# Four small moves between engines: zeroing, a product, a scaling and two factors in an attention and feed-forward kernel

## The chip, the core and the metric

The kernel runs on one core of a Trainium2 chip. The core has a matrix engine (TensorE, PE in the profile, with its weight loads shown apart as PEld), three engines that work on tiles element by element (VectorE, DVE; ScalarE, ACT; GpSimd, POOL) and a queue engine (SyncE, SP) that issues most transfers. Each engine works through its own list of instructions in order, and waits on semaphores for the others. Data lie in SBUF (128 partitions); TensorE writes its results to PSUM, from where VectorE or ScalarE take them.

The metric is the device time of one execution in microseconds (us), as the median of several runs. Lower is better.

## The reference

Two stages. The first is a linear attention with a decaying state, for 4 batches and 8 heads of 768 steps with 48 channels each; the second is a feed-forward block on the 3072 rows that come out, 384 wide, 1024 inside.

```python
def _attn_ref(r, k, v, w, u):
    ...
    for t in range(S):
        kt, vt, rt = (k[:, :, t], v[:, :, t], r[:, :, t])
        cur = np.einsum('bhd,bhe->bhde', u[None] * kt, vt)
        y[:, :, t] = np.einsum('bhd,bhde->bhe', rt, state + cur)
        state = w[None, :, :, None] * state + np.einsum('bhd,bhe->bhde', kt, vt)
    ...
def _moe_ref(x, w_in, w_out, g_ln):
    h = x @ w_in
    h_max = np.max(h, axis=-1, keepdims=True)
    e = np.exp(h - h_max)
    sm = e / (np.sum(e, axis=-1, keepdims=True) + 1e-09)
    solu = h * sm
    mu = np.mean(solu, axis=-1, keepdims=True)
    var = np.mean((solu - mu) ** 2, axis=-1, keepdims=True)
    ln = (solu - mu) / np.sqrt(var + 1e-06) * g_ln
    return (ln @ w_out).astype(np.float32)
```

`r`, `k`, `v`, `w`, `u` arrive in float32, the weights `w_in`, `w_out` and `g_ln` in float64. The part with `u` is what each step adds for itself; below it is called the own product: the sum over the channels of r times u times k, one number per head and step.

## The kernel before

**Chunks.** The 768 steps of each batch are cut into 6 chunks of 128. A chunk of one batch is a unit; there are 24, numbered 0 to 23, all batches of the first chunk first. A unit's `r`, `k` and `v` are loaded with the steps on the partitions (`rpad`, `kpad`, `vt`). The order of the instructions is written out by hand, for every engine: what a function issues stands on the engine's list where the function is called. Nothing reorders it.

**A unit's way.** `decay_k` (L718) multiplies `k` with a table of decays `kdec` on GpSimd and gives `kp`. `weigh` (L732) makes the own products on GpSimd in two multiplications, k times u (L734) and that times r (L735); `sum_own` (L737) sums them over the channels on VectorE; `diagonal` (L744) puts the sums on the diagonal of the score tile, on ScalarE for units 0 to 3 (L749), on GpSimd later (L754). `turn_r` and `turn_k` transpose `r` and `k` on TensorE; VectorE scales the first out of PSUM (L779), ScalarE copies the second (L788). `whole_scores` or `scores` multiplies the two on TensorE (L801, L819), `take_scores` puts the valid half of the result into the score tile on VectorE (L827, L832), and `whole_y` or `merged_y` multiplies that with `vt` (L858, L881). `take_y` (L892) copies the result to SBUF on ScalarE: it is the input `xT` of the feed-forward part. From unit 4 on, `vt` has two halves of 64 steps, with the running state in the rows that a half leaves free; so the second half, `vt[:, 1]`, must be zero where nothing is loaded. L641 zeroes it for all six `vt` tiles, on ScalarE, at the start.

**Feed-forward.** `ffn_in` (L962) multiplies with `w_in` on TensorE into one PSUM tile `h_ps` (L969); there is only one such tile, so the next unit's product waits until it has been read twice: by ScalarE's exponential (L977), and then by VectorE's L1053 in `unit_a`, which makes `solu` from it and the exponential. `unit_b` (L1057) takes sums of squares on ScalarE. Then come the variance, the root (`root`, L1075, on GpSimd) and two factors (`shifts`, L1079: a scale and a shift for each row), with which `normalise` (L1098, on ScalarE) finishes the row. `halve_ln` (L1124) splits its words into 16-bit halves on ScalarE and issues a transpose by DMA on SP; `join_ln` (L1130) puts the halves together again on VectorE (L1121). `row_sums_12` and `row_sums_34` make sums of the rows of two units (L1201 to L1207), and `both_a` to `both_d` multiply with `w_out`, two units at a time (L1211).

**The weights.** They arrive as float64 words and become float32 in 14 pieces, 0 to 5 of `w_in`, 6 to 13 of `w_out`. A piece takes four steps: `convert_a` (L531, ScalarE), `convert_b` (L540, VectorE, two instructions), `convert_c` (L556, GpSimd, L560), and for pieces of `w_out` `convert_d` (L563): a multiplication with `minus_g`, on VectorE (L571) for even pieces, on ScalarE (L568) for odd ones.

**The order around the change.** The start (L1313 to L1396) is written out. The transposes of unit 0 and of the decay table come first; ScalarE then copies the table out (`turn_table`, L665) and has in front of it the copy of `u` (L639) and the six zeroings (L641). On GpSimd come `ones` (L710), two small products `wide` (L1322) that wait for VectorE's tables, `weigh(0)`, `decay_k(0)`, and later `decay_k(1)` and `weigh(1)`. A loop of five turns follows (L1399, i from 2 to 6), in which every turn handles up to two pieces of `w_out`: the pieces taken up in one turn go through `convert_c` and `convert_d` in the next. Three more loops handle the middle, and the end (L1725 on) is written out again: there unit 23, the last, gets its `variance`, `root` and `shifts` alone, between the stages of units 18 to 22.

Of the kernel before, what the change touches and what calls it, by code (L numbers as in the profile page):

```python
# [9 lines left out]
F32 = mybir.dt.float32  # L10
# [389 lines left out]
def direct_path(  # L400
# [29 lines left out]
    nc = tc.nc  # L430
    B, H, S, D = r.shape
# [18 lines left out]
    apool = ctx.enter_context(tc.tile_pool(name="apool", bufs=2))  # L450
# [15 lines left out]
    NLD, NV = 5, 6  # L466
    rpads = [const.tile([128, H, P], F32, name=f"rpad{i}") for i in range(NLD)]
    kpads = [const.tile([128, H, P], F32, name=f"kpad{i}") for i in range(NLD)]
    vts = [const.tile([128, 2, H, P], F32, name=f"vt{i}") for i in range(NV)]

    def load(i, which="krv"):
        b, c = units[i]
        for t, src, n in ((kpads, k, "k"), (rpads, r, "r")):
            if n in which:
                nc.sync.dma_start(out=t[i % len(t)][:, :, 0:D],
                                  in_=src[b, :, ts(c, T), :].rearrange("h s d -> s h d"))
        if "v" in which:
            vt = vts[i % NV]
            for n, at, size in ((0, 0, T),) if i < WHOLE else ((0, 0, U), (1, U, U)):
                nc.sync.dma_start(  # L480
                    out=vt[at : at + size, n, :, 0:D],
                    in_=v[b, :, ds(c * T + at, size), :].rearrange("h s d -> s h d"))
# [57 lines left out]
    def convert_b(j):  # L540
        hi, low = step[j]
        n = low.shape[1]
        ma = wpool.tile([128, n], U32, tag="ma", name="ma", bufs=4)
        part = ma
        if pieces[j][2] is None:
            part = psM.tile([128, n], F32, tag="m", name="part").bitcast(U32)

        nc.vector.tensor_scalar(out=part, in0=hi, scalar1=3, scalar2=0x3FFFFFF8,  # L550
                                op0=ALU.logical_shift_left, op1=ALU.bitwise_and)
        nc.vector.scalar_tensor_tensor(out=ma, in0=hi, scalar=0xC0000000, in1=part,  # L552
                                       op0=ALU.bitwise_and, op1=ALU.bitwise_or)
        step[j] = ma, low
# [8 lines left out]
    def convert_d(j, scalar=False):  # L563
        dst, _, f = pieces[j]
        ma, low = step.pop(j)
        if f is not None:
            if scalar:
                nc.scalar.activation(out=dst, in_=ma.bitcast(F32), func=ACT.Copy,  # L568
                                     scale=minus_g[:, f : f + 1])
            else:  # L570
                nc.vector.tensor_scalar_mul(out=dst, in0=ma.bitcast(F32),  # L571
                                            scalar1=minus_g[:, f : f + 1])
# [64 lines left out]
    u_ps = psM.tile([128, dm], F32, tag="m", name="u_ps")  # L637
    nc.tensor.matmul(u_ps, ones_row, u_row, start=True, stop=True)
    nc.scalar.copy(out=u_bc.rearrange("p h d -> p (h d)"), in_=u_ps)  # L639
    for vt in vts:  # L640
        nc.scalar.activation(out=vt[:, 1].rearrange("p h x -> p (h x)"),  # L641
                             in_=ident[:, 0:1].to_broadcast([128, H * P]), func=ACT.Copy, scale=0.0)
    nc.vector.tensor_scalar(out=pw[:, 0, 0], in0=wd_ps, scalar1=LOW, scalar2=HIGH,
# [64 lines left out]

    ones = const.tile([128, 1], F32, name="ones")
    nc.gpsimd.memset(ones, 1.0)  # L710

    live = {}

# [4 lines left out]
    def decay_k(i):  # L718
        X = live.setdefault(i, {})
        X["kp"] = apool.tile([128, H, P], F32, name="kp", bufs=5)  # L720
        nc.gpsimd.tensor_mul(X["kp"].rearrange("p h d -> p (h d)"),  # L721
                             kpads[i % NLD].rearrange("p h d -> p (h d)"),
                             kdec.rearrange("p a d -> p (a d)"))
# [5 lines left out]
                             rpads[i % NLD].rearrange("p h d -> p (h d)"),  # L729
                             rdec.rearrange("p a d -> p (a d)"))  # L730

    def weigh(i, engine):  # L732
        rku = live[i]["rku"] = apool.tile([128, H, D], F32, name="rku")
        engine.tensor_mul(rku, kpads[i % NLD][:, :, 0:D], u_bc)  # L734
        engine.tensor_mul(rku, rku, rpads[i % NLD][:, :, 0:D])  # L735

    def sum_own(i):  # L737
        own = live[i]["own"] = small.tile([128, H, 1], F32, name="own")
# [35 lines left out]
    def turn_r(i):  # L774
        rT = factors(i)["rT"]
        ps = psM.tile([128, HP, T], F32, tag="m", name="tr_ps")
        for a in range(HP):
            nc.tensor.transpose(ps[:, a, :], pair(rpads[i % NLD], a), ident)
        nc.vector.tensor_mul(rT, ps, fore)  # L779
# [287 lines left out]
    def unit(i):  # L1067
        unit_a(i)
        unit_b(i)
# [9 lines left out]
    def shifts(i, j, engine):  # L1079
        i = max(i, SEVEN)  # L1080
        if i < j:
            tot, shift, scale, rstd = (stats[:, n, i:j] for n in (1, 2, 3, 4))
            engine.tensor_scalar(out=scale, in0=rstd, scalar1=-float(dff), scalar2=1.0,
                                 op0=ALU.mult, op1=ALU.mult)
            engine.tensor_tensor(out=shift, in0=tot, in1=rstd, op=ALU.mult)  # L1085
# [34 lines left out]
    def join(words, turned):  # L1120
        nc.vector.tensor_copy(out=words.bitcast(U16).rearrange("p n (t o) -> p o n t", o=2),  # L1121
                              in_=turned)
# [7 lines left out]
    def join_ln(i):  # L1130
        X = live[i]
        if i not in ROOM:
            X["lnT"] = fpool.tile([128, KF, 128], F32, name="lnT")
        else:
            X["lnT"] = bigs[ROOM[i]].rearrange("p (f t) -> p f t", f=KF)
        join(X["lnT"], X["turned"])
# [72 lines left out]
    def block(dst, rows, weights, start=False):  # L1209
        for f in range(KH):  # L1210
            nc.tensor.matmul(dst, rows[:, f], weights[:, f], start=(start and f == 0),  # L1211
                             stop=(f == KH - 1), skip_group_check=True)
# [52 lines left out]
    def both_c(i):  # L1265
        X, Y = live.pop(i), live.pop(i + 1)
        ending[i] = X
        o, o2, a, e = (X[n] for n in ("o", "o2", "a", "e"))
        rows, rows2 = (out[ds(b * S + c * T, T)] for b, c in (units[i], units[i + 1]))
        if not X.get("summed"):  # L1270
            nc.vector.tensor_tensor(out=o2[:, right], in0=a, in1=o2[:, right], op=ALU.add)
        block(a, Y["lnT"][:, KH:KF], sums_w[4])
        if i + 2 == N:
            nc.sync.dma_start(out=rows2[:, right], in_=o2[:, right])
        if X.get("summed") != 2:
            nc.vector.tensor_tensor(out=o[:, right], in0=e, in1=o[:, right], op=ALU.add)
        nc.sync.dma_start(out=rows, in_=o)
# [13 lines left out]
    def attend(chunks, at=0):  # L1291
        chunks = [i for i in chunks if i < N]
        scores(chunks, at)
        outer(chunks)
# [25 lines left out]
    for q in range(2):  # L1320
        rows = slice(q * P, q * P + D)
        nc.gpsimd.tensor_tensor(out=wide.rearrange("p (a q) -> p a q", q=2)[P : P + D, :, q],  # L1322
                                in0=back[rows, :, 0], in1=pw[rows, 0, 0], op=ALU.mult)
    weigh(0, nc.gpsimd)
    decay_k(0)
    sum_own(0)
    diagonal(0)
# [1 line left out]
    spin(2)  # L1329
    whole_scores(0)  # L1330
    convert_b(0)
    decay_k(1)
    weigh(1, nc.gpsimd)
    turn_r(1)
    spin(4)
# [63 lines left out]
    for i in range(LA, LA + LO):  # L1399
        j = i - LA  # L1400
        load(i + 5, "kr")
        load(i + 4, "v")
        if i > LA:
            ffn_in(j)
        before, now = now, [todo.pop(0) for _ in range(2 if todo else 0)]
        turn_r(i + 2)
        turn_k(i + 2)
        for p in before:
            convert_c(p)
        for p in now:  # L1410
            take_up(p)
        if i > LA:
            diagonal(i + 1)
            unit(j)
        for p in before:
            convert_d(p, p % 2)
        sum_own(i + 2)
        decay_k(i + 3)
        if i + 3 >= FIRST:
            decay_r(i + 3)  # L1420
        weigh(i + 3, nc.gpsimd)
        if i - LO >= 0:
            halve_ln(i - LO)
        if i - LO - 1 >= 0:
            join_ln(i - LO - 1)
        if i + 1 < WHOLE:
            whole_scores(i + 1)
            take_scores(i + 1)
        else:
            place(i + 1)  # L1430
            attend([i + 1])
            middle(i + 1)
        if LA < i < WHOLE:
            whole_y(i)
            take_y(i)
            whole_outer(i)
        elif i >= WHOLE:
            merged_y(i)
            take_y(i)
        if i > LA:  # L1440
            update(i)
        else:
            nc.vector.tensor_single_scalar(out=minus_g, in_=g_sb, scalar=-1.0, op=ALU.mult)
        if i + 1 >= WHOLE:
            take_scores(i + 1)
        for p in now:
            convert_b(p)
        halve_rk(i + 3)
# [17 lines left out]
    i = LA + LO  # L1466
    j, l = i - LA, 0
# [41 lines left out]
    for i in range(LA + LO + 2, ELEVEN, 2):  # L1509
        j, l = i - LA, i - LA - LO  # L1510
# [8 lines left out]
        first, second = ([n] if n < N else [] for n in (i + 2, i + 3))  # L1519
# [121 lines left out]
    for i in range(ELEVEN, N - 1, 2):  # L1641
        j, l = i - LA, i - LA - LO
        one, two = turned[i]
        first, second = ([n] if n < N else [] for n in (i + 2, i + 3))
# [80 lines left out]
    i = N - 1  # L1725
    j, l = i - LA, i - LA - LO
# [68 lines left out]
    variance(i, N, nc.vector)  # L1795
    root(i, N)
    both_c(l)
    shifts(i, N, nc.vector)
    join_ln(l + 3)
    row_sums_12(l + 2)  # L1800
    row_sums_34(l + 2, nc.vector)
    both_d(l)
# [72 lines left out]
```

## Time and profile before

| what | value |
|---|---|
| median of 5 runs | 322.94 us (321.71 to 323.35) |
| the profiled execution | 322.67 us, its span 320.9 us |
| granted TensorE clock | 0.998 |
| TensorE busy | 307.6 us (96%) |
| VectorE, ScalarE, GpSimd busy | 266.5 us (83%), 244.5 us (76%), 245.5 us (76%) |
| first product with `w_in` on TensorE (L969) | starts at 23.25 us |
| last matmul | ends at about 315 us |
| L641, zeroing on ScalarE | 6 of 0.62 us |
| L735, second own product on GpSimd | 24, median 1.01 us |
| L571, scaling on VectorE | 4, 0.47 to 0.73 us |
| L568, scaling on ScalarE | 4 of 0.60 us |

The profile is one execution. A line of its timeline gives the start in us from the begin of the span, the length in us, the engine, the line of the kernel, the operation, the tile written and the tiles read, their sizes, how many equal instructions were merged, and in brackets how long the engine was idle before and what ended that wait. "issue" stands for a wait for nothing that the profile shows.

### The profile page before, as it was taken

The page shows a single profiled execution, that of the slowest core. Times are in us where ns is not written, and L with a number is a line of the kernel's source. Part 1 is how long each engine was busy: PE and PEld are TensorE (multiplying, and loading weights), DVE is VectorE, ACT ScalarE, POOL GpSimd, SP SyncE. Part 2 cuts the span into 40 slices and gives each one's busy share as a digit, 9 for nine tenths or more (in the row PEclk, how much of TensorE's full clock was granted, in tenths as well). Part 3 has the DMA queues.
Part 4 walks back from the last instruction along what each step waited for, and adds up shares of the span by engine and source line. Part 5 has one row for each costly group of instructions (what it writes and reads, how often), then busy time and mean ns, then how long its engine had stood idle before and what let it go on. Part 6 is the DMA issues. An engine that isn't in the chain of part 4 may idle for free.

```text
span 320.9 us, 9696 instructions
## 1 busy us (share of the span) xinstructions
PE 307.6 (96%) x3903; PEld 217.1 (68%) x3903; DVE 266.5 (83%) x449; ACT 244.5 (76%) x418; POOL 245.5 (76%) x264
## 2 busy tenths in 40 slices
PE   5989999999999999999999999999999999999992
PEld 4966565555456466687677677667768677669892
DVE  7696999998887988989889799799979947677770
ACT  3885888888549888968968969949959968788420
POOL 4899778879999999999999999979988275272000
PEclk9999999999999999999999999999999999999999
DMA  8999998778999999988998999995876455575821
GB/s 172 246 257 194 206 183 198 132 134 143 190 165 179 172 171 154 162 146 171 161 201 170 173 182 218 206 194 87 163 182 140 78 133 116 128 198 118 189 89 61
DMA packets 165779, 52.62 MB, mean 164 GB/s; under 512 B 158301, under 2 KB 161502, under 8 KB 165726
## 3 DMA queue, kind: packets, MB, share of 16 engines
q1 hardware_dynamic: 165712, 51.92, 83.4%
q8 instruction: 32, 0.52, 0.7%
q14 instruction: 21, 0.17, 0.2%
q10 hardware_dynamic: 14, 0.00, 0.0%
HBM read 26.75 MB, written 4.72 MB: 98 GB/s over the span
## 4 chain that ended last, share of the span: by engine, by line
PE 64%; POOL 16%; DVE 11%; issue 4%; DMA 3%; POOLq 0%
PE o_ps L1211 26%; PE h_ps L969 18%; PE h_part L1003 9%; POOL kp L721 3%; POOL rku L734 3%; POOL rp L728 3%; POOL big L754 3%; PE y_ps L881 2%; PE at L819 2%; POOL rku L735 2%; DMA rpad<-in_r_dram 2%; DVE solu L1053 1%; PE h_part L881 1%; DVE ma L552 1%; PE y_ps L858 1%
## 5 line engine op out<-in xcount | busy, mean ns | idle before, releaser
L969 PE MATMUL h_ps<-w_in_sb,xT 128*128 128x512 f32 x216 | 96.9, 598 | 0.0
L969 PEld LDWEIGHTS h_ps<-w_in_sb,xT 128*128 128x128 f32 x216 | 39.9, 190 | 44.9 <-issue 42.9
L1127 ACT COPY halves<-solu 128x2048 uint16<-128x2048 uint16 x23 | 43.6, 1896 | 1.8 <-DMA halves<-halves 1.7
L721 POOL TENSOR_TENSOR kp<-kpad,kdec 128x512 f32<-128x512 f32 x24 | 34.1, 1423 | 1.3 <-ACT kdec L665 0.6
L1121 DVE COPY big<-halves 128x2048 uint16<-128x2048 uint16 x21 | 33.7, 1612 | 0.7 <-DMA halves<-halves 0.4
L1121 DVE COPY lnT<-halves 128x2048 uint16<-128x2048 uint16 x18 | 31.5, 1772 | 0.0
L735 POOL TENSOR_TENSOR rku<-rku,rpad 128x384 f32<-128x384 f32 x24 | 29.1, 1214 | 1.9
L832 DVE COPY_PREDICATED big<-later_half,at 64x512 f32<-64x512 uint32 x40 | 29.5, 736 | 0.7
L734 POOL TENSOR_TENSOR rku<-kpad,u_bc 128x384 f32<-128x384 f32 x24 | 29.8, 1240 | 0.2
L754 POOL TENSOR_SCALAR_AFFINE_SELECT big<-own 64x512 f32<-64x512 f32 x40 | 27.6, 691 | 1.8
L1211 PE MATMUL o_ps<-w_out_sb,ma 128*128 128x192 f32 x160 | 28.1, 328 | 0.0
L1211 PEld LDWEIGHTS o_ps<-w_out_sb,ma 128*128 128x128 f32 x160 | 26.2, 190 | 1.9 <-issue 1.6
L977 ACT ACTIVATE e<-h_ps 128x1024 f32<-128x1024 f32 x18 | 18.4, 1022 | 8.9 <-PE h_ps L969 8.8
L728 POOL TENSOR_TENSOR rp<-rpad,rdec 128x512 f32<-128x512 f32 x15 | 25.1, 1676 | 0.0
L1061 ACT ACTIVATE e<-solu,stats 128x1024 f32<-128x1024 f32 x20 | 22.9, 1147 | 2.2 <-DVE solu L1053 2.1
L1053 DVE SCALAR_TENSOR_TENSOR solu<-h_ps,stats,e 128x1024 f32<-128x1024 f32 x18 | 23.1, 1284 | 1.5
L1102 ACT ACTIVATE solu<-solu,stats 128x1024 f32<-128x1024 f32 x17 | 21.0, 1233 | 1.0 <-POOL stats L1085 0.9
L1166 PE MATMUL o_ps<-w_out_sb,lnT 128*128 128x384 f32 x64 | 21.6, 491 | 0.0
L1072 POOL TENSOR_SCALAR stats<-stats 128x2 f32<-128x2 f32 (+2 forms) x13 | 5.9, 452 | 19.3 <-ACT e L1061 18.7
L956 POOL TENSOR_TENSOR vt<-vt,wide 48x384 f32<-48x384 f32 x16 | 19.4, 1227 | 0.8
L1211 PE MATMUL o_ps<-w_out_sb,lnT 128*128 128x192 f32 x112 | 19.8, 330 | 0.0
L1211 PEld LDWEIGHTS o_ps<-w_out_sb,lnT 128*128 128x128 f32 x112 | 18.3, 190 | 1.7 <-issue 1.4
(198 smaller groups left out, 699.8 us busy)
## 6 DMA issues: line engine op xcount, KB each, us to landing
raw<-in_moe_w_out_dram SPq DMA_DIRECT2D x16, 384.0 KB, 4.0
kpad<-in_k_dram SPq DMA_DIRECT2D x24, 192.0 KB, 5.0
rpad<-in_r_dram SPq DMA_DIRECT2D x24, 192.0 KB, 5.4
vt<-in_v_dram SPq DMA_DIRECT2D x40, 96.0 KB, 3.7
raw<-in_moe_w_in_dram SPq DMA_DIRECT2D x7, 512.0 KB, 6.6
out_dram<-o SPq DMA_DIRECT2D x18, 192.0 KB, 3.3
raw<-in_moe_w_in_dram SPq DMA_DIRECT2D x10, 256.0 KB, 4.1
out_dram<-kp SPq DMA_DIRECT2D x5, 192.0 KB, 2.6
```

The costliest lines, as they stand in the source:

```text
L721: nc.gpsimd.tensor_mul(X["kp"].rearrange("p h d -> p (h d)"), kpads[i % NLD].rearrange("p h d -> p (h d)"), kdec.rearrange("p a d -> p (a ...
L728: nc.gpsimd.tensor_mul(X["rp"].rearrange("p h d -> p (h d)"), rpads[i % NLD].rearrange("p h d -> p (h d)"), rdec.rearrange("p a d -> p (a ...
L734: engine.tensor_mul(rku, kpads[i % NLD][:, :, 0:D], u_bc)
L735: engine.tensor_mul(rku, rku, rpads[i % NLD][:, :, 0:D])
L754: nc.gpsimd.affine_select(out=G[rows, c].rearrange("p a q u -> p (a q) u"), in_=X["own"][rows].to_broadcast([U, H, U]), compare_op=ALU.is_ ...
L832: nc.vector.copy_predicated(X["G"][rows, c].rearrange("p a q u -> p q a u"), later_half[rows].unsqueeze(1).to_broadcast([U, 2, HP, U]), X[ ...
L969: nc.tensor.matmul(h_ps[:, ts(n, NX)], X["xT"][:, j, :], w_in_sb[:, j, ts(n, NX)], start=(j == 0), stop=(j == KD - 1))
L1003: nc.tensor.matmul(dst, rows, weights, start=start, stop=True, skip_group_check=True)
L1053: nc.vector.scalar_tensor_tensor(out=solu, in0=X["h"], scalar=rs, in1=X["e"], op0=ALU.mult, op1=ALU.mult, accum_out=tot)
L1121: nc.vector.tensor_copy(out=words.bitcast(U16).rearrange("p n (t o) -> p o n t", o=2), in_=turned)
L1127: copy(out=both.rearrange("p (o n) -> p o n", o=2), in_=split(X["solu"]))
L1211: nc.tensor.matmul(dst, rows[:, f], weights[:, f], start=(start and f == 0), stop=(f == KH - 1), skip_group_check=True)
```

## The change

There are four edits.

- Of the six zeroings of `vt[:, 1]`, those of tiles 4 and 5 move from ScalarE to GpSimd, as two memsets behind `ones`.
- `weigh` can make its two products on two engines. For unit 0 the first stays on GpSimd, and the second goes to VectorE, behind the two scalings of the transposes of unit 0 (L779, L790). `decay_k(1)` moves ahead of `decay_k(0)` on GpSimd.
- `convert_d` is called for ScalarE only, so the scaling of pieces 6, 8, 10 and 12 moves from VectorE to ScalarE, next to that of pieces 7, 9, 11 and 13. It does so in the four turns of the loop with i from 3 to 6.
- Near the end, the two factors of the last unit (`shifts`) stand behind the second of two joins on VectorE (`join_ln(l + 3)`) instead of ahead of it.

TensorE's and SP's lists keep their order.

```diff
-    for vt in vts:
+    for vt in vts[:4]:
         nc.scalar.activation(out=vt[:, 1].rearrange("p h x -> p (h x)"),
                              in_=ident[:, 0:1].to_broadcast([128, H * P]), func=ACT.Copy, scale=0.0)
...
     ones = const.tile([128, 1], F32, name="ones")
     nc.gpsimd.memset(ones, 1.0)
+    for vt in vts[4:]:
+        nc.gpsimd.memset(vt[:, 1], 0.0)
...
-    def weigh(i, engine):
-        rku = live[i]["rku"] = apool.tile([128, H, D], F32, name="rku")
+    def weigh(i, engine, second=None):
+        rku = live.setdefault(i, {})["rku"] = apool.tile([128, H, D], F32, name="rku")
         engine.tensor_mul(rku, kpads[i % NLD][:, :, 0:D], u_bc)
-        engine.tensor_mul(rku, rku, rpads[i % NLD][:, :, 0:D])
+        (second or engine).tensor_mul(rku, rku, rpads[i % NLD][:, :, 0:D])
...
-    weigh(0, nc.gpsimd)
+    weigh(0, nc.gpsimd, nc.vector)
+    decay_k(1)
     decay_k(0)
     sum_own(0)
     diagonal(0)
...
     convert_b(0)
-    decay_k(1)
     weigh(1, nc.gpsimd)
...
         for p in before:
-            convert_d(p, p % 2)
+            convert_d(p, True)
         sum_own(i + 2)
...
     both_c(l)
+    join_ln(l + 3)
     shifts(i, N, nc.vector)
-    join_ln(l + 3)
     row_sums_12(l + 2)
```

## The prediction

> **What bounds the kernel now.** I read the page's busy times and slices first, then TensorE's timeline for every place where it stood still, then the rows of the engine that ended each such wait.
>
> ```profile
> PE 307.6 (96%) x3903; PEld 217.1 (68%) x3903; DVE 266.5 (83%) x449; ACT 244.5 (76%) x418; POOL 245.5 (76%) x264
> ...
> PE   5989999999999999999999999999999999999992
> ```
>
> From 23.25 us, where the first product with `w_in` starts, to 315 us, TensorE hardly stops. So an edit on another engine is worth only the TensorE waits it removes, plus what it takes off the start. TensorE's timeline shows these waits after 28 us (the bracket holds the idle time and what ended it); one more, 0.73 us at 213.5 with "issue" as its end, is not this change's.
>
> ```profile
> 58.25 0.57 PE L913 MATMUL kv_ps<-vt,kp 64*48 64x48 f32 x30 [0.65 <-DVE big L779]
> ...
> 67.43 0.57 PE L913 MATMUL kv_ps<-vt,kp 64*48 64x48 f32 x30 [0.67 <-DVE big L779]
> ...
> 74.75 0.69 PE L819 MATMUL at<-big 48*64 48x64 f32 x32 [0.32 <-DVE big L832]
> ...
> 128.53 1.54 PE L1211 MATMUL o_ps<-lows,ma 128*128 128x192 f32 x8 [0.31 <-DVE stats L1049]
> ...
> 298.88 1.54 PE L1211 MATMUL o_ps<-lows,ma 128*128 128x192 f32 x8 [0.57 <-DVE ma L1202]
> ```
>
> Their sum is 2.52 us: the most that the edits behind the start can give. Now part by part.
>
> **Start: two tiles zeroed on GpSimd, one product on VectorE, `decay_k(1)` first.** The timeline of the first 45 us:
>
> ```profile
> 7.13 3.22 ACT L641 ACTIVATE vt<-ident 128x512 f32<-128x512 f32 x6
> ...
> 9.28 1.00 POOL L735 TENSOR_TENSOR rku<-rku,rpad 128x384 f32<-128x384 f32 x1
> ...
> 10.26 0.57 ACT L665 COPY kdec<-kd_ps 128x512 f32<-128x512 f32 x1
> ...
> 10.90 2.52 POOL L721 TENSOR_TENSOR kp<-kpad,kdec 128x512 f32<-128x512 f32 x2 [0.61 <-ACT kdec L665]
> ...
> 17.25 0.66 PE L778 MATMUL tr_ps<-ident,rpad 128*128 128x128 f32 x4
> ...
> 18.18 0.69 DVE L779 TENSOR_TENSOR big<-tr_ps,tab 128x512 f32<-128x512 f32 x1
> 18.79 1.35 DVE L827 COPY_PREDICATED big<-later,at 128x512 f32<-128x512 uint32 x2
> ```
>
> ScalarE issues six zeroings, 0.54 us apart. Without two, its queue reaches the copy of `kdec` at 9.2 us, but TensorE's transposes for it end at 9.47, so it starts at about 9.53 instead of 10.26: 0.73 us earlier. GpSimd takes the two zeroings after its `ones` (done at 3.90) and before `wide`, which waits for VectorE until 7.67. A 128x128 memset took 0.19 us there, a 128x1 one 0.09; by the slope between these a 128x512 one costs 0.5 us, by four times the whole row 0.8. Both together cost 1.0 to 1.6 us of a gap of 3.77: nothing. Without that gap, `wide` and all behind it on GpSimd would move by that much. SP's loads of these two tiles wait for GpSimd now instead of ScalarE, but are issued after 28 us.
>
> The second product (1.0 us on GpSimd) on VectorE costs between the 0.35 us of its 128x192 additions and the 0.69 us of its 128x512 ones; I take 0.53, nearest by size. It starts behind L790 at 9.35, GpSimd's first product being done at 9.21, so `own` of unit 0 ends at 10.4 instead of 10.87, and ScalarE's eight diagonals follow 0.45 earlier. GpSimd, ready at 9.21, waits for `kdec` until 10.17 and then makes `kp` of unit 1, then of 0 (needed at 15.7, made at 12.7). Its queue stays 0.73 ahead: `rku` of unit 1 ends at 14.75, and VectorE's L739 starts at 14.85, when L827 lets go, instead of 15.51.
>
> How much of that reaches TensorE? VectorE goes on 0.66 earlier until L779 of unit 2, which reads the transposes that TensorE ends at 17.91. TensorE had no wait of note from 6.65 to there, so this time stays. L779 moves from 18.18 to 17.97; L827, `whole_y(1)` and 23.25 follow. Bounds: 0 (TensorE's 0.49 us of "issue" at 21.06 could absorb it) and 0.73 (all). I take 0.20, the end of TensorE's row.
>
> The Trainium skill, "SBUF — State Buffer", section "Who interferes with whom", speaks against this edit: a VectorE instruction with two SBUF inputs contends with a GpSimd one that reads SBUF. Here GpSimd waits for `kdec` while the product runs, so I add nothing; if they collided, by that rule one would wait for the other's whole length, and the start's gain would go. The same section lets a GpSimd zeroing, which only writes, pass such instructions; no run here shows that yet.
>
> **`convert_d` wholly on ScalarE.** Pieces 6, 8, 10, 12 of the weights leave VectorE: L571 at 41.55, 50.34, 59.51 and 68.87, holding it for 0.65, 0.57, 0.57 and 0.39 us to the next start, 2.18 in all. ScalarE gains four more of L568 (0.60 each, 0.51 between starts). VectorE's and ScalarE's timelines of one turn of the loop:
>
> ```profile
> 58.30 1.28 DVE L1053 SCALAR_TENSOR_TENSOR solu<-h_ps,stats,e 128x1024 f32<-128x1024 f32 x1
> ...
> 59.51 0.65 DVE L571 TENSOR_SCALAR w_out_sb<-ma,minus_g 128x384 f32<-128x384 f32 x1
> ...
> 67.67 1.28 DVE L1053 SCALAR_TENSOR_TENSOR solu<-h_ps,stats,e 128x1024 f32<-128x1024 f32 x1
> ```
>
> ```profile
> 59.63 1.15 ACT L1064 ACTIVATE solu<-solu,stats 128x1024 f32<-128x1024 f32 x1 [0.85 <-DVE solu L1053]
> ...
> 61.86 0.60 ACT L568 ACTIVATE w_out_sb<-ma,minus_g 128x384 f32<-128x384 f32 x1
> ...
> 66.20 1.02 ACT L977 ACTIVATE e<-h_ps 128x1024 f32<-128x1024 f32 x1
> ```
>
> At 41.55 the 0.65 us mostly vanish: the next L779 (48.34) waits for TensorE, and the product L1053 for ScalarE's exponential; 0.10 remain. With the 0.57 of 50.34, L1053 at 58.30 moves 0.67 earlier, and the TensorE wait at 58.25 goes. But ScalarE has no gap from 59.63 to its next exponential at 66.20, and now carries one more L568 in it: the exponential moves by 0.67 - 0.51 = 0.16 only. L1053 at 67.67 waits for it, and the next `h_ps` product (69.01) needs the buffer that L1053 empties. So the two waits of 0.65 and 0.67 are replaced by a wait on this chain; of 1.32 us TensorE keeps 0.16. Bounds: -0.51 (L1053 not earlier, the extra L568 wholly in the path) and 1.32 (the exponential not late).
>
> At 68.87, 0.39 us go behind that L1053; L832, which TensorE waits for at 74.75, ends 0.16 + 0.39 earlier. The wait of 0.32 goes. ScalarE's next exponential comes up to 0.35 later, with its product wanted by TensorE only 2.7 us afterwards (78.3 against 80.99).
>
> GpSimd works without a gap from 66.80 (L560, freed by VectorE's L552) to 121.2. That L552 comes 0.67 + 0.57 = 1.24 earlier, so GpSimd's whole stretch does too; VectorE waits for its end at 121.25, and this is what makes TensorE stop at 128.53. GpSimd gains more than TensorE's 0.16 + 0.32, so the 0.31 go. Bounds for each of these two waits: 0 and its size.
>
> The same section of the skill has VectorE's `tensor_scalar` from SBUF able to lock out GpSimd for its whole length, and ScalarE wait for nobody. L571 took 0.47 to 0.73 us here, L568 0.60 each time, in keeping with it; by the rule GpSimd's stretch would gain up to another 0.39 us, which changes nothing as the 0.31 are gone already.
>
> **`shifts` of the last unit behind the second join.**
>
> ```profile
> 295.81 0.16 DVE L1083 TENSOR_SCALAR stats<-stats 128x1 f32<-128x1 f32 x1 [0.40 <-POOL stats L1076]
> ...
> 295.95 1.33 DVE L1121 COPY big<-halves 128x2048 uint16<-128x2048 uint16 x1
> ...
> 304.88 1.32 DVE L1121 COPY big<-halves 128x2048 uint16<-128x2048 uint16 x1
> ```
>
> The join no longer stands behind the wait of 0.40 us: it starts at 295.41, the shifts follow at 296.75, and L1202 ends 0.33 earlier; TensorE resumes at 298.55. Behind the shifts is ScalarE's L1102 (296.84), which now starts at 297.0, 0.15 later; its copy, its DMA transpose and the join at 304.88 (which waits for the transpose: its last landing is at 304.86) come 0.15 later too. That join's sums are next wanted by TensorE at 308.20, and end at 307.81, with 0.15 to the matmul: 307.96. So 0.24 remain. Bounds: 0 (a late landing) and 0.57.
>
> **Sum.** 0.20 + 0.16 + 0.32 + 0.31 + 0.24 = 1.23 us. The profiled execution took 322.67 us (span 320.9, 1.8 around it), 0.27 below the median of the runs, 322.94. It would be 321.4, and the median 321.7. About 0.3% (0.97 us) is what a measurement of this kernel can tell from no change.
>
> **Rivals.**
> 1. *The start gives all of its 0.73.* The chain of waits names GpSimd's `kp` and `rku` there, which speaks for it; TensorE's gapless row to 17.91 against. 321.7 - 0.53 = 321.2.
> 2. *ScalarE takes the place of VectorE.* The gapless 59.63 to 66.20 speaks for it, VectorE's earlier L1053 against. -0.51 in place of 0.16: 322.4.
> 3. *Hidden anyway.* Only the start's 0.20 reaches the end, because the waits at 74.75, 128.53 and 298.88 reappear behind other work. Each had one named cause that this change moves, which speaks against it. 322.7.
> 4. *Slower.* The four added L568 lie in ScalarE's path in all four turns, between `h_ps` and the next exponential, at 0.51 each: 2.04 less the 0.20 of the start, 324.8. It decides where a turn leaves ScalarE less than 0.51 idle; the rows show 1.01, 0.80, 0.85 and 1.15 before its waits.
>
> **How the numbers follow.** Forecast 0.45 (own range 321.3 to 322.1, four fifths of it faster by over 0.3%), rivals 0.17, 0.15, 0.15 and 0.08. Faster 0.36 + 0.17 = 0.53, within 0.3% 0.09 + 0.30 = 0.39, slower 0.08. The range leaves out rival 4 and a start or an end at its best with both 0.65 waits gone: 320.5 to 323.0.
>
> **What would show it.** `kdec` at about 9.5 and L779 of unit 2 at about 18.0; no 0.65 wait at 58 but `h_ps` near 68.7 instead of 69.01; no waits at 74.4 and 128; the late stop cut to about 0.25. The prediction is wrong if TensorE's first `h_ps` product is not earlier, if ScalarE's exponential near 66 is late, or if a new stop of TensorE appears.

## The result and the profile after

The changed kernel took 321.48 us (median of 38 runs, 319.79 to 326.1), the kernel before 322.59 us on the same chips (64 runs): ratio 0.9957, interval 0.9944 to 0.9969. That is 0.43% faster, or 1.39 us with 1.0 to 1.8 as its interval; the forecast was 1.23 us, a median of 321.7 in a range of 320.5 to 323.0. A ratio, here and below, is taken over the executions that were not in a longer, slower state, and it is not the quotient of the two medians, which are 1.11 us apart here. Sign and size are right. Of the five terms of the sum, one was hardly a term at all in this pair of profiles, and the others are not all made as the prediction had it.

The page of the changed kernel first: the busy times, TensorE's row of the slices, and one line of the DMA queues (packets, MB, share of 16 engines), which the prediction had not read.

```profile
PE 306.7 (96%) x3903; PEld 216.7 (68%) x3903; DVE 261.2 (82%) x446; ACT 245.8 (77%) x420; POOL 248.3 (78%) x265
...
PE   6979999989999999999999999999999999999990
...
q8 instruction: 33, 0.54, 0.7%
```

VectorE lost 5.3 us of work, ScalarE and GpSimd gained 1.3 and 2.8, and the span went from 320.9 to 320.2 us. The timeline of the start (from which engine, line and tile; the bracket holds the idle time and what ended it):

```profile
3.85 0.99 POOL L712 MEMSET vt<- 128x512 f32 x2
...
6.96 2.18 ACT L641 ACTIVATE vt<-ident 128x512 f32<-128x512 f32 x4
...
9.34 0.59 ACT L665 COPY kdec<-kd_ps 128x512 f32<-128x512 f32 x1 [0.19 <-PE kd_ps L664]
...
9.43 0.56 DVE L737 TENSOR_TENSOR rku<-rku,rpad 128x384 f32<-128x384 f32 x1 [0.25 <-POOL rku L736]
...
17.35 0.69 DVE L781 TENSOR_TENSOR big<-tr_ps,tab 128x512 f32<-128x512 f32 x1
...
17.96 1.35 DVE L829 COPY_PREDICATED big<-later,at 128x512 f32<-128x512 uint32 x2
...
19.37 0.86 PE L860 MATMUL y_ps<-big,vt 128*32 128x128 f32 x24
...
21.53 0.30 PE L860 MATMUL y_ps<-big,vt 128*32 128x128 f32 x2 [1.30 <-issue]
...
23.23 5.42 PE L971 MATMUL h_ps<-w_in_sb,xT 128*128 128x512 f32 x12
```

The moved work costs what was said: 0.99 us for two zeroings, 0.56 for the product, `kdec` at 9.34. L781 of unit 2 came 0.83 us earlier, more than the 0.21 of the forecast. Then TensorE stood for 1.30 us where it had stood 0.49, with "issue" as the end of the wait. This is its line in the kernel before:

```profile
21.55 0.30 PE L858 MATMUL y_ps<-big,vt 128*32 128x128 f32 x2 [0.49 <-issue]
```

The first product with `w_in` began at 23.23 as it had at 23.25: in this pair nothing of the start was left.

TensorE's timeline in the turn that the prediction worked out, and then the other engines' in the same turn:

```profile
57.58 0.57 PE L915 MATMUL kv_ps<-vt,kp 64*48 64x48 f32 x30 [0.29 <-DVE big L781]
...
66.19 0.92 PE L915 MATMUL kv_ps<-vt,kp 64*48 64x48 f32 x32 [0.16 <-ACT xT L894]
67.80 1.10 PE L883 MATMUL y_ps<-big,vt 112*32 112x64 f32 x64 [0.69 <-ACT big L790]
68.86 5.42 PE L971 MATMUL h_ps<-w_in_sb,xT 128*128 128x512 f32 x12
74.20 0.69 PE L821 MATMUL at<-big 48*64 48x64 f32 x32
```

```profile
57.63 1.28 DVE L1055 SCALAR_TENSOR_TENSOR solu<-h_ps,stats,e 128x1024 f32<-128x1024 f32 x1
...
61.20 1.11 ACT L568 ACTIVATE w_out_sb<-ma,minus_g 128x384 f32<-128x384 f32 x2
...
65.73 1.00 POOL L560 TENSOR_TENSOR ma<-ma,lows 128x384 uint32<-128x384 uint32 x1 [0.56 <-DVE ma L552]
...
66.05 1.02 ACT L979 ACTIVATE e<-h_ps 128x1024 f32<-128x1024 f32 x1
...
67.51 1.28 DVE L1055 SCALAR_TENSOR_TENSOR solu<-h_ps,stats,e 128x1024 f32<-128x1024 f32 x1
```

VectorE's L1055 starts 0.67 us earlier at 57.63, the exponential only 0.15 earlier at 66.05, and the `h_ps` product 0.15 earlier at 68.86: the wait moved from VectorE's `big` to ScalarE's, as forecast. The stop at 74.4 is gone, and so is the one at 128. The end:

```profile
293.43 1.32 DVE L1123 COPY big<-halves 128x2048 uint16<-128x2048 uint16 x1
...
294.82 0.15 DVE L1085 TENSOR_SCALAR stats<-stats 128x1 f32<-128x1 f32 x1
...
296.63 1.57 PE L1213 MATMUL o_ps<-lows,ma 128*128 128x192 f32 x8 [0.22 <-ACT kp L1230]
...
302.90 1.33 DVE L1123 COPY big<-halves 128x2048 uint16<-128x2048 uint16 x1 [0.41 <-DMA halves<-halves]
...
313.31 1.99 SPq L1287 DMA_DIRECT2D out_dram<-kp  x1
```

The join goes ahead of the factors, TensorE's stop before L1213 shrinks from 0.57 to 0.22 us, and the second join waits 0.41 for its transpose without holding TensorE. The last line is a loss of this execution: SP's last DMA issue took 1.99 us instead of 0.52, as SP's timeline of the kernel before has it:

```profile
315.60 0.52 SPq L1285 DMA_DIRECT2D out_dram<-kp  x1
```

With it the time from the last matmul to the end was 7.30 instead of 5.75 us. In another execution of the same kernel it was 5.91. So the span understates this pair: the matmuls ended 2.29 us earlier.

### The profile page after: what moved, and what is told of

Read it like the earlier page. It is cut to its first block, busy times and chain, and to the rows that moved or that the text cites. A ratio compares the mean times of both kernels' runs of the same rounds, so it can differ in the third digit from the quotient of the medians.

```text
span 320.2 us, 9697 instructions
## 1 busy us (share of the span) xinstructions
PE 306.7 (96%) x3903; PEld 216.7 (68%) x3903; DVE 261.2 (82%) x446; ACT 245.8 (77%) x420; POOL 248.3 (78%) x265
## 4 chain that ended last, share of the span: by engine, by line
PE 68%; POOL 17%; DVE 9%; issue 4%; ACT 0%; POOLq 0%; ACTq 0%
PE o_ps L1213 26%; PE h_ps L971 18%; PE h_part L1005 9%; POOL rp L730 3%; POOL big L756 3%; POOL rku L736 3%; POOL kp L723 3%; PE y_ps L883 2%; PE at L821 2%; POOL rku L737 1%; PE at L803 1%; PE y_ps L860 1%; DVE solu L1055 1%; PE h_part L883 1%; PE tr_ps L780 1%
## 5 line engine op out<-in xcount | busy, mean ns | idle before, releaser
L1123 DVE COPY big<-halves 128x2048 uint16<-128x2048 uint16 x21 | 32.8, 1567 | 1.0 <-DMA halves<-halves 0.7
L1123 DVE COPY lnT<-halves 128x2048 uint16<-128x2048 uint16 x18 | 30.7, 1723 | 0.7 <-DMA halves<-halves 0.6
L737 POOL TENSOR_TENSOR rku<-rku,rpad 128x384 f32<-128x384 f32 x23 | 28.3, 1231 | 1.8
L1213 PE MATMUL o_ps<-w_out_sb,ma 128*128 128x192 f32 x160 | 28.1, 328 | 0.0
L1213 PEld LDWEIGHTS o_ps<-w_out_sb,ma 128*128 128x128 f32 x160 | 26.2, 190 | 1.9 <-issue 1.8
L730 POOL TENSOR_TENSOR rp<-rpad,rdec 128x512 f32<-128x512 f32 x15 | 26.2, 1747 | 0.0
L1055 DVE SCALAR_TENSOR_TENSOR solu<-h_ps,stats,e 128x1024 f32<-128x1024 f32 x18 | 23.1, 1284 | 1.5
L1168 PE MATMUL o_ps<-w_out_sb,lnT 128*128 128x384 f32 x64 | 21.5, 489 | 0.0
L958 POOL TENSOR_TENSOR vt<-vt,wide 48x384 f32<-48x384 f32 x16 | 19.4, 1228 | 0.8
L1213 PE MATMUL o_ps<-w_out_sb,lnT 128*128 128x192 f32 x112 | 19.8, 330 | 0.0
L1213 PEld LDWEIGHTS o_ps<-w_out_sb,lnT 128*128 128x128 f32 x112 | 18.2, 190 | 1.7 <-issue 1.4
```

Source lines behind the costliest of these rows:

```text
L730: nc.gpsimd.tensor_mul(X["rp"].rearrange("p h d -> p (h d)"), rpads[i % NLD].rearrange("p h d -> p (h d)"), rdec.rearrange("p a d -> p (a ...
L737: (second or engine).tensor_mul(rku, rku, rpads[i % NLD][:, :, 0:D])
L1055: nc.vector.scalar_tensor_tensor(out=solu, in0=X["h"], scalar=rs, in1=X["e"], op0=ALU.mult, op1=ALU.mult, accum_out=tot)
```

## The experiments

What had to be settled: whether the stop with "issue" at 21.5 us takes whatever the start edits give (theory F, of a fixed arrival: TensorE waits there for instructions that come when they come), or something else makes it; what each of the three edits gives alone; and whether ScalarE's chain is what limits the second one. All ten traces have the same 3903 matmuls in the same order (one experiment drops 26 idle ones), so that each can be laid over the kernel before, matmul by matmul.

**Both kernels again, and each edit alone.** These two kernels are unchanged:

> The kernel before, profiled once more. TensorE stood still twice with no cause that the profile shows: 0.49 us, ending at 21.55, and 0.73 us, ending at 214.23 us; in the changed kernel the first was 1.30 us and ended at 21.53, and the second was absent. Theory F: these are waits for TensorE's own instructions, which arrive by DMA in pieces of 16 KB; the first lies at the same place of the program in every execution and ends near 21.5 us, the second depends on when its piece happens to arrive, and may be absent, other in length or elsewhere this time. Rival C: the second stop belongs to the kernel before and its absence to the change, so it is here again with about 0.7 us at 214.

> The changed kernel, profiled once more. Theory F: TensorE stops again before the same weight load (the 230th, in whole_y of unit 1) if it gets there before 2.2 to 2.5 us after the first 16 KB transfer on the instruction queue has begun, as in every execution so far; the transfer began anywhere from 18.0 to 19.4 us, so the stop is 0 to 1.3 us this time and the first product with w_in between 22.2 and 23.3. A stop of 0.4 to 0.8 us near 213 (before the 2942nd weight load) may be there or not. Rival C: the profile repeats, 1.3 us at 20.2 and no stop at 213.

Each of the other three is the kernel before with one part of the change. The start alone:

```diff
-    for vt in vts:
+    for vt in vts[:4]:
...
+    for vt in vts[4:]:
+        nc.gpsimd.memset(vt[:, 1], 0.0)
...
-    weigh(0, nc.gpsimd)
+    weigh(0, nc.gpsimd, nc.vector)
+    decay_k(1)
     decay_k(0)
...
-    decay_k(1)
```

> The kernel before with the edits of the start alone (two zeroings on GpSimd, the second product of unit 0 on VectorE, decay_k(1) first). Both theories: kdec's copy at about 9.3 and VectorE's L779 (here L781) of unit 2 at about 17.35 instead of 18.18. Theory F: TensorE reaches its stop about 0.8 us earlier and leaves it at the same 21.5, so the first product with w_in starts at 23.2 as before, and the median is within 0.2 us of before. Rival S (the start's gain reaches the end, as the prediction had it with 0.20 and its first rival with 0.73): the first product with w_in at 23.05 to 22.5, and 0.2 to 0.7 us off the median.

The scaling alone:

```diff
-            convert_d(p, p % 2)
+            convert_d(p, True)
```

> The kernel before with all scalings of w_out on ScalarE, alone. Theory A (the prediction's steps): ScalarE's chain from the square sums to the next exponential takes the place of VectorE's, so the h_ps product at 69.01 moves by 0.16 only, the scores at 74.75 by 0.5, and the matmul at 128.53 by 0.8; 0.8 us off the median. Rival V: VectorE alone was the bound, both stops of 0.65 and 0.67 go for good, h_ps near 67.8 and 1.5 to 2 us off the median. Rival N: the moves are given back between 130 and 290 us, no change of the median beyond 0.3 us.

The factors behind the second join alone:

```diff
-    shifts(i, N, nc.vector)
     join_ln(l + 3)
+    shifts(i, N, nc.vector)
```

> The kernel before with the last unit's two factors behind the second join, alone. Theory E (the prediction's step): TensorE's stop before L1211 at 298.88 falls from 0.57 to about 0.25 us, the last unit's transpose lands 0.15 later, and the sums behind it take a little of the gain back; 0.25 us off the median. Rival: the whole of the stop goes, 0.4 to 0.57 us. Second rival: the late transpose costs TensorE a new stop near 308 us and nothing is left.

Measured against the kernel before on the same chip (322.41 us): start 322.91, ratio 0.9992 (0.9963 to 1.0022); scaling 322.0, ratio 0.9971 (0.9943 to 0.9999); factors 323.0, ratio 1.0 (0.9967 to 1.0033). In the one further execution of each, the kernel before took 322.24, and the changed one 321.03 on another chip, where the kernel before had a median of 323.06. The intervals of start and factors hold both nothing and the forecast; only the scaling is told from no change, and barely. The traces say more. The table gives, for each execution, how much later (+) or earlier (-) TensorE was than in the first profile of the kernel before: at two places in us, and then the step from place to place (times are those of the kernel before). The last three rows are the experiments told below.

| execution | resumed at 21.55 | at 33.5 | step at 49.1 | to 68.0 | to 74.8 | to 128.5 | to 221 | to 306 |
|---|---|---|---|---|---|---|---|---|
| before, again | -0.69 | -0.13 | -0.21 | +0.02 | -0.02 | +0.05 | -0.23 | -0.01 |
| factors alone | +0.09 | +0.05 | +0.69 | 0.00 | -0.03 | +0.05 | +0.07 | -0.43 |
| scaling alone | -1.10 | -0.41 | -0.30 | +0.18 | -0.38 | -0.32 | -0.07 | +0.07 |
| start alone | -0.63 | -0.67 | -0.30 | +0.01 | -0.03 | 0.00 | -0.16 | +0.24 |
| changed | -0.02 | -0.06 | -0.30 | +0.20 | -0.38 | -0.34 | -1.00 | -0.44 |
| changed, again | -0.64 | -0.68 | -0.29 | +0.28 | -0.39 | -0.32 | -0.07 | -0.43 |
| changed, load 3 from ScalarE | +0.06 | +0.02 | -0.30 | +0.17 | -0.38 | -0.35 | -0.06 | +0.11 |
| changed, no idle matmuls | none | +0.37 | -0.30 | +0.19 | -0.38 | -0.34 | -0.15 | -0.39 |
| changed, piece 10 on VectorE | +0.53 | +3.68 | -0.30 | -0.30 | 0.00 | +0.04 | -0.06 | -0.41 |

Read by columns, each edit has places of its own:

*The start.* Where TensorE resumes is not set by the edits: 0.69 earlier in an execution of the unchanged kernel, 0.02 earlier with the whole change. It follows the instruction queue of the page (q8: 33 transfers of 16 KB each). The first of these began at 19.1, 18.5, 18.0 and 19.4 us in the four executions without the start edits, and at 19.1, 18.5, 18.6, 19.2, 18.8 and 19.6 in those with them. Seven executions stopped, for 0.49 to 1.59 us, always before the same weight load, the trace's 221st (the expectations call it the 230th, because they also count entries of that list that are no weight loads), and went on 2.24 to 2.48 us after the transfer's begin. The three others (the kernel before, again; scaling alone; no idle matmuls) reached that place 2.36 us or more after it and did not stop. Start alone stopped for 0.88 us. Theory F as first put, with an end near 21.5 us in every execution, was wrong: start alone went on at 20.92, and its first product with `w_in` came at 22.62. The end follows the begin of the transfer. The start edits bring TensorE to the place earlier, and do not set the end of the stop.

But the second column shows what they are worth. Without them, executions that resumed 0.69 and 1.10 early kept only 0.13 and 0.41 of it; with them, 0.64 and 0.63 were kept whole. The weight loads of TensorE (PEld) say why. In the kernel before, again, and then in the changed one, again, both of which resumed at 20.9:

```profile
27.22 0.30 PEld L969 LDWEIGHTS h_ps<-w_in_sb,xT 128*128 128x128 f32 x2 [0.92 <-POOL w_in_sb L560]
...
31.74 0.42 PEld L786 LDWEIGHTS tk_ps<-ident,kp 128*128 128x128 f32 x4 [0.26 <-POOL kp L721]
```

```profile
27.02 0.19 PEld L971 LDWEIGHTS h_ps<-w_in_sb,xT 128*128 128x128 f32 x1 [0.24 <-issue]
...
31.15 0.46 PEld L788 LDWEIGHTS tk_ps<-ident,kp 128*128 128x128 f32 x4
```

In the first, TensorE came early and waited for GpSimd, which was still putting `w_in` together; in the second GpSimd is 0.6 us ahead and no such wait is there. So the start edits gave 0.55 us (0.68 less 0.13) between two executions in which the transfer began at 18.5, and 0.06 to 0.03 between those in which it began at 19.1 to 19.4.

*The scaling.* It takes away the wait for VectorE's L779 at 49.1 (0.30 us of delay in the first profile, 0.09 and 1.0 in the two others without start or scaling edits; the start edits alone take it away as well), then costs 0.17 to 0.28 us by 68.0, and then gives 0.38 at 74.8 and 0.32 to 0.35 at 128.5. All kernels with the whole edit agree in this, and those without it have next to nothing in these columns. Theory A had asked for 0.16, 0.5 and 0.8 us at 69.0, 74.8 and 128.5; from 33.5 on, the scaling alone gave 0.12, 0.50 and 0.82. Its timeline of TensorE:

```profile
57.22 0.57 PE L913 MATMUL kv_ps<-vt,kp 64*48 64x48 f32 x30 [0.28 <-DVE big L779]
...
67.43 1.10 PE L881 MATMUL y_ps<-big,vt 112*32 112x64 f32 x64 [0.68 <-ACT big L788]
...
73.83 0.69 PE L819 MATMUL at<-big 48*64 48x64 f32 x32
```

Of the first 0.65 us 0.28 remain, the second wait is there in full with ScalarE in VectorE's place, and the third is gone.

*The factors.* At 298.9, each of the six executions with this edit gains 0.33 to 0.36, and some 0.08 more behind it. The last column of the run with load 3 from ScalarE hides this, because it lost 0.5 us at one more stop with "issue" at 220.9, 2.46 us after the begin of a transfer. TensorE's timeline with this edit alone:

```profile
49.82 0.57 PE L913 MATMUL kv_ps<-vt,kp 64*48 64x48 f32 x30 [0.76 <-DVE big L779]
...
299.36 0.92 PE L1211 MATMUL o_ps<-lows,ma 128*128 128x192 f32 x4 [0.23 <-ACT kp L1228]
```

The late stop is cut to 0.23, as in the changed kernel. The first line is why this execution was no faster than the kernel before: VectorE happened to be late there, far from the edit.

**Piece 10 back on VectorE.** The changed kernel with one of the four moved scalings where it was, the one that lengthens ScalarE's gapless stretch:

```diff
-            convert_d(p, True)
+            convert_d(p, p != 10)
```

> The changed kernel with piece 10 alone back on VectorE (the turn of the loop in which ScalarE had no gap). Theory A (ScalarE's chain is what bounds the turn): its exponential near 66.05 and VectorE's product behind it come 0.5 earlier, the h_ps product at 68.86 moves by 0.4 to 0.5, GpSimd's stretch from 65.7 on starts 0.5 later than in the changed kernel, and the median is 0.2 to 0.5 us below it. Rival V (VectorE is what bounds it): the scaling holds up VectorE by 0.57, h_ps at 68.86 stays or is later, median 0 to 0.5 us above the changed kernel. The start differs from run to run by up to 0.8 us, so the distance from TensorE's transposes at 47.2 to that product counts.

322.13 us, ratio 0.9979 (0.9953 to 1.0005). TensorE's timeline:

```profile
70.52 0.57 PE L915 MATMUL kv_ps<-vt,kp 64*48 64x48 f32 x30 [0.68 <-DVE big L781]
...
77.83 0.69 PE L821 MATMUL at<-big 48*64 48x64 f32 x32 [0.32 <-DVE big L834]
...
131.65 1.54 PE L1213 MATMUL o_ps<-lows,ma 128*128 128x192 f32 x8 [0.31 <-DVE stats L1051]
```

By 68.0 this kernel gains 0.30 where the changed one loses 0.20: the difference is 0.50, the 0.51 us between two of ScalarE's L568. So ScalarE's chain is what limits TensorE there, as the prediction had it. But with VectorE and so GpSimd held by this one instruction again, the stops at 74.4 and 128.5 are back, and 0.72 us are lost for 0.50 gained. By the traces the whole edit is the better one by 0.2 us; the 0.2 to 0.5 us below the changed kernel that theory A expected of the median did not come.

Its profiled execution was a long one (325.21 us) for another reason, which its windows show (its first line names the columns: the window and its length, the busy time of each engine with the number of instructions, the granted clock, the DMA share and GB/s):

```profile
core 0: us, PE busy (x) PEld busy (x) DVE busy (x) ACT busy (x) POOL busy (x), PEclk, DMA share, GB/s
...
20.00:22.08 2.08, 0.49 (x21) 0.31 (x10) 2.01 (x4) 0.13 (x1) 1.27 (x2) 0.98 1.15 235
22.08:27.00 4.92, 4.92 (x70) 3.50 (x70) 4.45 (x9) 3.94 (x11) 4.29 (x5) 0.50 0.77 134
27.00:32.00 5.00, 5.00 (x11) 2.04 (x9) 0.79 (x2) 0.00 (x0) 4.92 (x5) 0.82 1.07 233
```

The transfer began at 19.6, and the stop lasted 1.59 us. Then TensorE ran at half its clock, by the trace's record of the clock from 21.99 to 28.82 us (the 0.82 of the last line is a mean with 1.8 us at half in it), which cost 3.15 us (from +0.53 to +3.68 in the table).

**Without the idle matmuls.** The changed kernel has 13 matmuls in the `spin` calls at four places of its start (26 in the trace) whose result nothing reads. Without them 26 more of the useful weight loads stand ahead of the place of the stop in TensorE's list, and might last until the transfer.

```diff
-    spin(2)
...
-    spin(4)
...
-    spin(3)
...
-    spin(4)
```

> The changed kernel without the 13 idle matmuls that keep TensorE busy between its first transposes and whole_y of unit 1 (26 weight loads fewer; the three at the very start stay). They compute nothing that is used. Theory F (the stop is at an instruction of TensorE's list, and lasts until a transfer has landed): the stop moves 26 weight loads later in the work, into whole_outer of unit 1, still ends about 2.4 us after the transfer's begin, and the first product with w_in is 0.3 to 0.5 us earlier for the same begin. Rival W: the idle matmuls hold TensorE's clock up; without them its matmuls between 10 and 23 us take up to twice as long, and the first product with w_in is later than 23.5. Rival P: the stop stays before whole_y's 29th matmul, so it belongs to that work and not to the list.

321.66 us, ratio 0.9961 (0.994 to 0.9982), the same as the changed kernel. TensorE's timeline:

```profile
13.51 2.29 PE L860 MATMUL y_ps<-big,vt 128*32 128x128 f32 x30 [1.75 <-issue]
...
20.00 1.51 PE L860 MATMUL y_ps<-big,vt 128*32 128x128 f32 x30 [1.04 <-ACT big L790]
```

No stop at the 221st load is left, but TensorE was idle for 1.75 us at 11.8 and the 30 matmuls behind it took 2.29 us instead of 1.10; the granted clock was 0.67 from 12 to 17 us. The first product with `w_in` came at 22.92. The second bracket, 1.04 us, is a wait for ScalarE. So the first stop settles nothing here: TensorE came too late for it. From the begin of the transfer to that product it is 4.10 us, as in the changed kernel (4.09), and not the 0.3 to 0.5 less of theory F; the slower matmuls are those of rival W.

The second stop of this kind, near 214 us, does settle whether the place belongs to the list or to the work. In the kernel before, and then without the idle matmuls:

```profile
214.23 0.64 PE L881 MATMUL y_ps<-big,vt 128*32 128x64 f32 x28 [0.73 <-issue]
```

```profile
213.96 0.30 PE L883 MATMUL y_ps<-big,vt 128*32 128x64 f32 x2 [0.54 <-issue]
```

With 28 matmuls of the same product behind the stop, and then with 2, it moved by just the 26 that were taken out of the list. So this stop is tied to a place of TensorE's list and not to the work that is there, which speaks against rival P at the first stop too.

**Load 3 from ScalarE's queue, later.** Is the transfer of the instructions late because SP's queue is full of loads? The loads of `k` and `r` of unit 3 leave it:

```diff
-    load(3, "kr")
...
     take_up(2, 0)
+    load(3, "kr", nc.scalar)
     spin(4)
```

> The changed kernel with the two loads of unit 3's k and r (2048 pieces of 192 bytes) issued by ScalarE after its second copy of unit 2, at about 18.7 us, instead of by SP at 14 to 17 us. Theory D (the instruction transfer begins late because the queues are full of loads): it begins at 18.0 or earlier, ends TensorE's stop by 20.4, and the first product with w_in starts at 22.2 to 22.5; 0.5 to 0.9 us off the changed kernel. Rival T (its begin does not depend on these loads): 18.5 to 19.4 as in the others, first product near 23. Rival L: the late loads, or their issue on ScalarE (1 to 2 us), hold up kp of unit 3 or the copies of ScalarE, and the first product with w_in or the scores of unit 3 (32.5) come later.

321.95 us, ratio 0.9966 (0.9945 to 0.9986): nothing gained on the changed kernel. TensorE's timeline:

```profile
21.61 0.30 PE L859 MATMUL y_ps<-big,vt 128*32 128x128 f32 x2 [1.21 <-issue]
```

The transfer began at 19.2, as in the changed kernel (19.1), and not at 18.0 or earlier. In this one execution the two loads were not what held it up. What sets its begin between 18.0 and 19.6 stays open.

**The step at 213 to 221.** The 1.00 us there in the first profile of the changed kernel is not the change: in the other execution it is 0.07. Two chances meet. One is a second stop of the same kind, 0.20 to 0.77 us long in six of the ten executions, which ended 2.33 to 2.69 us after the begin of a transfer on the instruction queue; in the four others TensorE came there 2.32 us or more after it. The other is a race between VectorE's join and a product of GpSimd. The timelines of the two engines in the kernel before, and in the changed one:

```profile
212.32 2.45 DVE L1121 COPY big<-halves 128x2048 uint16<-128x2048 uint16 x1
...
212.30 1.29 POOL L728 TENSOR_TENSOR rp<-rpad,rdec 128x512 f32<-128x512 f32 x1
```

```profile
211.47 1.55 DVE L1123 COPY big<-halves 128x2048 uint16<-128x2048 uint16 x1
...
211.75 2.37 POOL L730 TENSOR_TENSOR rp<-rpad,rdec 128x512 f32<-128x512 f32 x1
```

Whichever starts first takes its 1.3 to 1.55 us, and the other some 1.1 more than it would alone. In two of the ten executions VectorE was first, by 0.28 us (one of the kernel before, one of the changed one), in eight GpSimd, by 0.02 to 0.08. Where GpSimd was first and no stop with "issue" came ahead, TensorE waited about 0.70 us for VectorE's `lnT` (three executions, among them the second of the changed kernel, at 215.9); the first profile of the changed kernel had neither of these two.

## Why the prediction was right, and where its steps were not

**Start, 0.20.** The zeroings (0.5 us each, hidden in GpSimd's gap), the product (0.56 against 0.53), `kdec` (9.34 against 9.53) and that they were ready on time were right. "TensorE had no wait of note from 6.65 to there, so this time stays" failed: TensorE was 0.59 us earlier by its row at 12.16 and 0.81 by 19.6, so more than 0.20 was at hand. TensorE's timelines of the kernel before, of the changed one and of the kernel before, again, one line of each:

```profile
10.26 1.97 PE L801 MATMUL at<-big 48*64 48x128 f32 x32
```

```profile
10.08 1.56 PE L803 MATMUL at<-big 48*64 48x128 f32 x32
```

```profile
13.34 0.66 PE L786 MATMUL tk_ps<-ident,kp 128*128 128x128 f32 x4 [0.25 <-POOL kp L721]
```

The first two are the same 32 matmuls. They took 1.25 to 1.97 us in the ten executions, with the edits or without, and 1.09 for the next unit. The trace's record of the granted clock begins, with the full clock, at 12.25 us in the first profile and at 10.2 to 11.8 in the others, so a lower clock until then is the likely reason; no row shows it. So 0.59 of the 0.81 came from a row that the edits leave alone, and 0.22 from behind it, near the term. The last line shows what the edits spare an early TensorE: the three executions without them in which it was 0.62 to 1.16 us early at 12.16 waited 0.21 to 0.48 us for GpSimd's `kp` there; none with them did.

And "L827, `whole_y(1)` and 23.25 follow" failed too, at the stop with "issue", which the prediction had only as a lower bound: it took the 0.81 whole. With a first `h_ps` product at 23.23 instead of 23.25, a sign that the prediction itself had named for being wrong was there in this pair. What the term was worth in the traces is 0 or 0.55, by when the instructions came, and 0.20 lies between; the run of the start alone, 0.3 us faster with an interval from 1.2 faster to 0.7 slower, can't fix its mean.

**ScalarE's chain, 0.16.** In the first pair of profiles the numbers are those of the forecast: L1055 0.67 earlier, the exponential 0.15, `h_ps` 0.15. But TensorE had been 0.36 earlier at 49.1, because a wait for L779 there had gone; from there to 68.0 it lost 0.20. TensorE's row at that place, in the kernel before and in the changed one:

```profile
48.77 0.88 PE L913 MATMUL kv_ps<-vt,kp 64*48 64x48 f32 x32
```

```profile
48.71 0.54 PE L915 MATMUL kv_ps<-vt,kp 64*48 64x48 f32 x32
```

The wait lies inside the 0.88 us and has no bracket, and so the prediction's list of waits lacked it. Its step "the next L779 (48.34) waits for TensorE" was a misreading: the transposes that L779 reads had ended at 47.89, and VectorE came late. In the changed kernel L781 does wait for them, by 0.32. The wait at 58.25 did not go; 0.29 of its 0.65 remained. The net is 0.10 where VectorE was 0.30 late at 49.1, more where it was later still, and a loss where it was nearly in time (0.18 between the two executions that resumed at 20.9: 0.08 gained, 0.26 lost). The mechanism, that ScalarE takes VectorE's place and the extra 0.51 lies in its path, was right, and rival 2's -0.51 too much.

**74.75 and 128.53, 0.32 and 0.31.** Measured 0.38 and 0.34 in the first pair and within 0.03 of that in every execution with the whole edit. The step that GpSimd's stretch starts 1.24 earlier was nearly so (L560 at 65.73 instead of 66.80, 1.07). That both hang on the scalings on VectorE and not on chance is shown by the scaling alone, which lacks them, and by the run with piece 10 on VectorE, which has them back.

**The late stop, 0.24.** 0.36 at the stop and 0.44 with what follows it; 0.43 with the edit alone. The 0.15 that the prediction took off for the later transpose did not come: the second join did wait for its transpose, by 0.41 us, but its sums were ready when TensorE wanted them.

**The sum.** In the first pair, without the chance at 213: 0.06 + 0.30 - 0.20 + 0.38 + 0.34 + 0.44 = 1.32 us. In the two executions that both resumed at 20.9, on two chips, the matmuls ended 1.26 us apart and the times 1.21. Both agree with the 1.39 us of the ratio, with quite different parts: in the first the start gave nothing, in the second 0.55. That the total came out as forecast is partly luck: in the first pair a late stop that gave 0.2 more than its term, and stops at 74.8 and 128.5 that gave 0.09 more, made up for a start and a chain of ScalarE that gave 0.2 less.

**The rivals.** Rival 1 (the start gives all) is near what the pair with early instructions shows, with 0.55 for its 0.73. Rival 3 (hidden anyway) was right about the start in the first pair and wrong about the three stops. Rival 4 (ScalarE late in all four turns) did not come: only the turn without a gap lost, some 0.2. "Not this change's", of the wait at 213.5, was right.

## What to carry to other kernels

When the idle time ahead of an instruction ends with "issue" and lasts over a few tenths, look at the instruction queue's transfers before counting on what lies ahead of it: work that is done earlier may only lengthen such a stop, and its gain depends on an arrival that varies from run to run. Follow the moved work to the next engine that waits behind the stop as well; here GpSimd's lead was what kept the gain of an early arrival. And lay several executions of both kernels over each other, instruction by instruction, before a step of 0.3 us is put down to an edit: in one pair alone a chance of 1.0 us and two steps of opposite sign looked like part of the change.

## What the runs showed of the hardware

- While the kernel runs, 32 or 33 transfers of 16 KB each go over the instruction queue. In seven executions TensorE stopped for 0.49 to 1.59 us at the same weight load, and went on 2.24 to 2.48 us after the begin of the first of them. A second stop of this kind moved by 26 weight loads when 26 were taken out of the list ahead of it. That TensorE waited for just these instructions is inferred from the times and the place; no row names the wait.
- A stop of 1.59 us was once followed by half the clock for 6.8 us, one of 1.75 us lay in a stretch of 5 us with a mean clock of 0.67; after stops of 1.20 to 1.30 us in three executions the clock stayed at 1.00, and the first `w_in` product came 1.70 us later. The Trainium skill, "TensorE: Matmul & The Clock Gate", Part 1, speaks of at least one idle window of about 3.4 us before the clock halves; here the clock halved after stops of about half that length.
- Of VectorE's join and a product on GpSimd that met, both from SBUF to SBUF, the one that started first made the other some 1.1 us longer, and a lead of 0.02 us was enough for GpSimd. The Trainium skill, "SBUF — State Buffer", section "Who interferes with whom", says that between a VectorE copy in a two-port mode and GpSimd, whoever issues first gets the shared ports for the whole instruction. The ten traces agree with it, with 1.52 to 1.55 us for a join that came first and 2.39 to 2.45 for one that came second; that the join runs in such a mode is not shown.
